# Chunked attention followed by a two-layer channel MLP: W1 loaded in four column quarters, an earlier release of the values loads, copies of turned keys and queries spread over steps, and the last tile computed by columns

## The chip, the cores and the metric

The kernel runs on one core of one Trainium2 chip. The metric is the device time of one execution in microseconds (us), as the median of several executions.

## What is computed

q, k and v have 4 batches, 8 heads, 768 positions and 64 features, in float32. First comes attention in chunks of 32 queries; each chunk sees 8 memory keys of its head, 16 positions to its left, itself, and 8 positions to its right. The heads are then put side by side (x has 4 x 768 rows of 512), and an MLP over a layer norm is added to x:

```
for c in range(nc):                       # 24 chunks of 32 queries
    l_start, r_end = max(0, c_start - 16), min(S, c_end + 8)
    k_full = concat([mem_k, k[:, :, l_start:r_end]])
    v_full = concat([mem_v, v[:, :, l_start:r_end]])
    scores = scale * q_c @ k_full^T
    out[:, :, c_start:c_end] = softmax(scores) @ v_full
...
xn = (x - mean(x)) / sqrt(var(x) + 1e-06) * g_ln
out = x + relu(xn @ w_ch1) @ w_ch2        # w_ch1 512 x 2048, w_ch2 2048 x 512
```

## The kernel before

**Tiles and units.** The 3072 rows of x are cut into 24 tiles of 128 rows, six to a batch. Three tiles make a unit, so there are eight units. The loop over the units is at L464. One unit is 16 "up" steps and then 12 "down" steps. An up step (L302) makes 128 of the 2048 hidden features for all 384 rows: four matmuls of 384 columns, one for each block of 128 input features, and a relu that puts the result into the tile rT. The relu of an even step runs on VectorE (L315), that of an odd step on ScalarE (L313). A down step (L319) does four of the 16 matmuls that make one output tile, each with 512 columns. After the fourth part, VectorE scales the sum by rstd and adds x (L331), and SyncE stores the tile (L334, 256 KB). The layer norm's factor rstd goes in only there; the matmuls work on (x - mean) * g.

**Attention is woven into the steps of the unit before.** While unit u runs, the attention of unit u+1's tiles is worked out. The dictionary `plan`, filled by `at(step, function, ...)` (L469), says after which step a piece of it is issued, and `attend` (L472) places three pieces for each tile. `scores` (L224) is eight matmuls of 128 columns and two exponentials on ScalarE (L237); `values` (L243) is 16 matmuls and VectorE's normalisation (L256 to L266); `turn_x` (L281) is four transposes on TensorE and a copy into xT on ScalarE (L289). `root` (L270), a square on ScalarE and a power on GpSimd, comes one step after `turn_x`.

**Turning keys and queries.** Scores need keys and queries with the features on the partitions. `kq_block` (L206) does this for two pairs of heads: 32 transposes for the keys and 32 for the queries on TensorE (L176, 16 for one pair of heads), then the copies out of PSUM, those of the keys by VectorE into KT (`keep_k`, L191), those of the queries by ScalarE into QZ (`keep_q`, L201). All copies of a block are issued together, keys of both pairs first, then queries of both. Batch 0 is special: its first 64 row groups of 96 are turned at the head of the program, a pair of heads at a time (L426 to L441), and the remaining third in unit 0 (steps 11 and 14). Batch 1 is turned in unit 1 (steps 2 and 6), batches 2 and 3 in units 2 and 4 (steps 19 and 22).

**PSUM.** There are two slots named att, of two banks each, and four named mm, of one bank. `slot` (L80) hands them out in turn. A matmul that is to write a slot waits until the slot's last reader is done.

**What sets the order.** Each engine runs its instructions in the order in which the program writes them (`manual_schedule`, L39). Waits between engines are put in by the framework, from which bytes of which tile an instruction reads and writes. GpSimd (POOL) issues all loads that change the type from float32 to float16: keys and queries (`load_kq`), values (`load_v_group`, `load_v_head`), W1 (`load_w1`), W2 (`load_w2`) and the memory values of batches 1 to 3. Each of these issues occupies POOL for 0.5 to 1.5 us; from the ninth on, each first waits for the landing of the eighth load before it. SyncE (SP) issues the loads and copies that keep the type: the memory keys and values, `v_mem`, `v_around`, the row g_row with g_ln, and the stores.

**The head of the program.** VectorE writes the zeros and ones that QZ, KT and V need (`clear_q` L341, `clear_k` L337, `clear_v` L344; the last ends with two copies from the tile `counts`, which put the mask of the first and the last window into V). The loads of V into a tile wait for `clear_v` of that tile. The order of loads on POOL is: first 64 row groups of K and Q of batch 0 in four loads; V groups 0 to 3 and 4, 5; W1's columns 0 to 512, 512 to 1024 and 1024 to 2048 (L399 to L401); the memory values; the remaining 32 row groups ("tails") of K and of Q; W2's blocks 0 and 1; V groups 6, 7; W2's block 2; V groups 8 to 11; W2's block 3. W1 lies in two tiles `w1c` of 1024 columns each. `stay_busy` (L294) issues matmuls on a tile of zeros between the first tiles' attention stages, whose results nobody reads.

Of the kernel before, what the change touches and what calls it, by code (L numbers as in the profile page):

```python
# [11 lines left out]
ALU = mybir.AluOpType  # L12
# [3 lines left out]
def kernel(  # L16
# [12 lines left out]
    nc = tc.nc  # L29
# [3 lines left out]
    NG = 12  # L33
# [59 lines left out]
    def as16(t):  # L93
        return t.bitcast(FP16)
# [4 lines left out]
    def load_kq(b, which, lo=0, hi=96, h0=0, h1=H):  # L99

        dst, src = ((k16, k), (q16, q))[which]
        nc.gpsimd.dma_start(
            out=dst[b % 2][lo:hi, h0:h1, :, :],
            in_=dram(src, (b * H + h0) * HS + 512 * lo,
                     [[512, hi - lo], [HS, h1 - h0], [1, 512]]),
        )
# [30 lines left out]
    def load_w1(lo, hi):  # L137
        c = lo // 1024
        nc.gpsimd.dma_start(
            out=w1c[c][:, :, lo - 1024 * c : hi - 1024 * c],  # L140
            in_=dram(moe_w_ch1, lo, [[FF, 128], [128 * FF, 4], [1, hi - lo]]),
        )

    def load_w2(c):

        nc.gpsimd.dma_start(
            out=w2c[c], in_=dram(moe_w_ch2, c * 512 * 512, [[2048, 128], [1, 2048]])
        )
# [48 lines left out]
    def keep_q(copy, pv, b, j, par, n, g0, g1):  # L197


        rows = slice(64 * par, 64 * par + 64)  # L200
        copy(  # L201
            out=free(QZ[b % 2][rows, j, g0, par, :], 0, [[128, g1 - g0], [8, 8], [1, 8]]),
            in_=free(pv[rows, :], 8 * g0, [[8, g1 - g0], [1, 8], [n, 8]]),
        )

    def kq_block(b, j, g0, g1, kind):  # L206

        pk, pq = slot("att"), None
        if kind == "att":
            pq = slot("att")  # L210
            pq = [pq[:, i, :] for i in range(2)]
        else:
            pq = [slot("mm")[:, :] for i in range(2)]
        for i in range(2):
            turn_kq(as16(pk[:, i, :]), k16[b % 2], j + i, 96)
        for i in range(2):
            turn_kq(as16(pq[i]), q16[b % 2], j + i, 96)
        for i in range(2):
            keep_k(as16(pk[:, i, :]), b, j + i, 96, g0 + 1 if g0 else 0, g1)
        for i in range(2):  # L220
            for par in range(2):
                keep_q(nc.scalar.copy, as16(pq[i]), b, j + i, par, 96, g0, g1)

    def scores(b, t):  # L224
        p = slot("att")
# [93 lines left out]
    def down(t, i, part):  # L319
# [9 lines left out]
        if part == 3:  # L329
# [3 lines left out]
            )  # L333
            nc.sync.dma_start(out=out[t // 6, 128 * (t % 6) : 128 * (t % 6) + 128, :], in_=o)  # L334


    def clear_k(i):  # L337
        nc.vector.memset(KT[i][:, :, 8:24], 0.0)
# [2 lines left out]
    def clear_q(i, par):  # L341

        nc.vector.memset(QZ[i][64 - 64 * par : 128 - 64 * par, :, :, par, :], 0.0)  # L343

    def clear_v(i):

        nc.vector.memset(V[i][0:32, 0, :, 0:64], 0.0)
        nc.vector.memset(V[i][64:96, NG - 1, :, 0:64], 0.0)
        nc.vector.memset(V[i][:, 1 : NG - 1, :, 64:65], 1.0)
        for c, g in enumerate((0, NG - 1)):  # L350
            nc.vector.tensor_copy(
                out=free(V[i][:, g, 0, 64:65], 0, [[HD, H]]),
                in_=free(counts[:, c : c + 1], 0, [[0, H]]),
            )
# [21 lines left out]
    nc.scalar.copy(out=memk16, in_=memk32)  # L376
    nc.scalar.copy(out=memv16[:, 0, :, 0:64], in_=memv32.rearrange("p (h d) -> p h d", h=H))
    stay_busy(10)
    for par in range(2):
        clear_q(0, par)  # L380
    clear_k(0)
    clear_v(0)
    mem_keys()
    mem_cols(0)
    stay_busy(5)
# [11 lines left out]
    nc.gpsimd.tensor_tensor(out=band[:, 1:2], in0=band[:, 1:2], in1=zero2[:, 1:2], op=ALU.add)  # L397
    for g in range(4, 6):
        load_v_group(0, g)  # L399
    load_w1(0, 512)  # L400
    load_w1(512, 1024)  # L401
    load_w1(1024, 2048)
    nc.gpsimd.dma_start(
        out=memv16[:, 1:B, :, 0:64],
        in_=dram(mem_v, H * 512, [[64, 8], [512, (B - 1) * H], [1, 64]]),
    )
    load_kq(0, 0, CUT, 96)
    load_kq(0, 1, CUT, 96)
    load_w2(0)
    load_w2(1)  # L410
    for g in range(6, 8):
        load_v_group(0, g)
    load_w2(2)
    for g in range(8, NG):
        load_v_group(0, g)
    load_w2(3)
# [29 lines left out]
    stay_busy(4)  # L446
    values(0, 0, 0)
    scores(0, 2)
    stay_busy(1)
    values(0, 1, 1)  # L450
    stay_busy(2)
    values(0, 2, 2)
    stay_busy(3)
    turn_x(0, 0, 0, "mm")
    stay_busy(4)
    turn_x(0, 1, 1, "mm")
    stay_busy(4)
    turn_x(0, 2, 2, "mm")
    for t in range(3):
        root(t, t)  # L460
# [3 lines left out]
    for u, tiles in enumerate(units):  # L464
        n = len(tiles)
        following = units[u + 1] if u + 1 < len(units) else []
        plan = {}

        def at(step, fn, *args):  # L469
            plan.setdefault(step, []).append((fn, args))  # L470

        def attend(steps):  # L472

            for i, (s0, s1, s2) in enumerate(steps):
                t = following[i]
                at(s0, scores, t // 6, t % 6)
                at(s1, values, t // 6, t % 6, t % 9)
                at(s2, turn_x, u + 1, i, t % 6)
                at(min(s2 + 1, 27), root, t % 6, t % 9)

        if u == 0:
            at(1, clear_q, 1, 0)
            at(5, clear_q, 1, 1)
            at(8, clear_v, 1)
            at(11, clear_k, 1)
            for j in (0, 2):
                at(11 + 3 * (j // 2), kq_block, 0, j, 6, NG, "att")
            for which in range(2):
                at(12, load_kq, 1, which)
            for g in range(6):  # L490
                at(15, load_v_group, 1, g)
            attend(((16, 19, 22), (17, 21, 24), (19, 23, 27)))
            at(26, mem_cols, 1)
            at(26, v_mem, 1)
        elif u == 1:
            for j in (0, 2):
                at(2 + 2 * j, kq_block, 1, j, 0, NG, "att")
            for g in range(6, NG):
                at(0, load_v_group, 1, g)
            for which in range(2):  # L500
                at(1, load_kq, 2, which)
            attend(((11, 16, 20), (15, 18, 23), (19, 22, 26)))
        elif following:
            steps = [(1 + 7 * i, 5 + 7 * i, 11 + 7 * i) for i in range(3)]
            if u in (2, 4):
                steps[2] = (15, 19, 22)
            attend(steps)
            if u in (2, 4):
                b = u // 2 + 1
                for j, step in ((0, 19), (2, 22)):  # L510
                    at(step, kq_block, b, j, 0, NG, "mm")
                for h in range(H):
                    at(2 + 2 * h, load_v_head, b, h)
                at(21, mem_cols, b)
                at(21, v_mem, b)
                at(22, v_around, b)
            if u == 3:
                for which in range(2):
                    at(2 + which, load_kq, 3, which)
        for step in range(16 + 4 * n):  # L520
            if step < 16:
                up(u, n, step)
            else:
                i, part = divmod(step - 16, 4)
                if u == 0:
                    d = step - 16
                    i, part = divmod(d, 2) if d < 6 else (d % 3, d // 3)
                down(tiles[i], i, part)
            for fn, args in plan.get(step, ()):
                fn(*args)  # L530

# [29 lines left out]
```

The softmax here doesn't subtract the row's maximum and nothing guards it: scores larger than these inputs give would overflow.

## Time and profile before

| | |
|---|---|
| median of 9 executions | 237.03 us (236.57 to 241.75) |
| the profiled execution: its own time | 237.09 us |
| its span, first to last instruction | 235.3 us |
| granted TensorE clock over the span | 0.996 |
| TensorE (PE) busy | 221.9 us, 94% |
| weight loads (PEld) busy | 135.9 us, 58% |
| VectorE (DVE) busy | 124.6 us, 53% |
| ScalarE (ACT) busy | 119.5 us, 51% |
| GpSimd (POOL) busy | 63.6 us, 27% |

By stretches of the span, TensorE is busy 9.9 of the first 12 us (of which much is the filler), 11.0 of the next 14, 32.6 of the 34 from 26 to 60, 48.3 of the 50 from 60 to 110, 49.4 of the 50 from 110 to 160, all of the 50 from 160 to 210, and 20.7 of the last 25.3.

How to read the profile's lines: L307 is line 307 of the kernel; PE is TensorE's matmuls, PEld its weight loads, which run beside the matmuls; "out<-in" names the tiles written and read. In a timeline line the first number is the start in us and the second the length of a group of instructions of one kind; the bracket tells how long the engine was idle just before and what ended that. In the list of waits, the three numbers are the total in us, the count, and the longest.

### The profile page before, as it was taken

The numbers are of one execution on the slowest core, as the hardware profiler recorded it, in microseconds if no ns is written. First come the engines' busy times: TensorE is split into PE (matmuls) and PEld (weight loads), VectorE is DVE, ScalarE is ACT, GpSimd is POOL, SyncE is SP. The second block draws the span as 40 slices with busy tenths as digits, with TensorE's granted clock in tenths as the row PEclk, the third lists the DMA queues.
The fourth block names the chain that finished last, engine by engine and source line by source line (L and its number), as shares of the span: only waits on it lengthen the run. The fifth ranks groups of instructions, "written<-read, shape, count | busy, mean of one in ns | idle before, by whom it ended". The sixth has DMA issues, their size and how long they took to land.

```text
span 235.3 us, 5407 instructions
## 1 busy us (share of the span) xinstructions
PE 221.9 (94%) x2251; PEld 135.9 (58%) x2251; DVE 124.6 (53%) x287; ACT 119.5 (51%) x227; POOL 63.6 (27%) x122
## 2 busy tenths in 40 slices
PE   7868999989899999989999999989999999999992
PEld 2544676547665577655764576656764676457540
DVE  6636773577735556384654365484644365434121
ACT  3663657455964456576572357576462457233200
POOL 6874156736400262303011344201011101110000
PEclk9999999999999999999999999999999999999998
DMA  4999999999998196942961193942001200110011
GB/s 77 193 126 208 201 193 175 169 201 225 106 153 171 49 119 12 73 88 54 201 109 45 51 120 10 94 64 92 0 3 45 89 3 0 46 57 34 0 71 64
DMA packets 44224, 22.30 MB, mean 95 GB/s; under 512 B 32376, under 2 KB 39928, under 8 KB 44152
## 3 DMA queue, kind: packets, MB, share of 16 engines
q0 software_dynamic: 39744, 14.38, 74.9%
q1 hardware_dynamic: 4456, 7.59, 10.7%
q8 instruction: 17, 0.28, 0.5%
q14 instruction: 7, 0.06, 0.1%
HBM read 29.10 MB, written 6.29 MB: 150 GB/s over the span
## 4 chain that ended last, share of the span: by engine, by line
PE 75%; DMA 9%; DVE 6%; issue 5%; ACT 3%; DVEq 0%
PE mm L307 33%; PE mm L324 30%; DMA w1c<-in_moe_w_ch_dram 6%; PE att L230 4%; PE att L176 3%; DMA V<-in_v_dram 3%; PE att L249 3%; DVE KT L191 2%; ACT QZ L201 2%; PE att L284 2%; DVE QZ L343 1%; DVE osb L331 1%; DVE xs L257 1%; PE mm L176 1%; ACT xT L289 0%
## 5 line engine op out<-in xcount | busy, mean ns | idle before, releaser
L307 PE MATMUL mm<-xT,w1c 128*128 128x384 f16 x512 | 90.3, 327 | 2.9 <-ACT xT L289 1.3
L324 PE MATMUL mm<-w2c,rT 128*128 128x512 f16 x384 | 89.0, 379 | 0.0
L307 PEld LDWEIGHTS <-w1c 128*128 128x128 f16 x512 | 56.1, 115 | 26.9 <-issue 2.1
L324 PEld LDWEIGHTS <-rT 128*128 128x128 f16 x384 | 35.6, 98 | 37.4
L315 DVE TENSOR_SCALAR rT<-mm 128x384 f16<-128x384 f32 x64 | 35.1, 556 | 33.0 <-PE mm L307 33.0
L313 ACT ACTIVATE rT<-mm 128x384 f16<-128x384 f32 x64 | 31.1, 490 | 40.3 <-PE mm L307 39.8
L331 DVE SCALAR_TENSOR_TENSOR osb<-mm,rstd,xs 128x512 f32<-128x512 f32 x24 | 18.0, 750 | 47.3 <-PE mm L324 25.9
L275 POOL TENSOR_SCALAR veps<-squares 128x1 f32<-128x1 f32 x24 | 4.6, 191 | 120.3 <-ACT junk L272 120.0
L237 ACT ACTIVATE AT<-att,band 96x512 f16<-96x512 f32 x48 | 30.1, 678 | 9.8 <-PE att L230 9.8
L289 ACT COPY xT<-att 128x512 f16<-128x512 f16 x21 | 12.3, 584 | 32.4 <-PE att L284 32.3
L112 POOL DMA_DIRECT2D V<-in_v_dram x24 | 18.5, 773 | 14.4 <-DMA V<-in_v_dram 5.2
L191 DVE COPY KT<-att 128x80 f16<-128x80 f16 (+3 forms) x44 | 18.3, 483 | 2.4 <-PE att L176 2.4
L266 DVE SCALAR_TENSOR_TENSOR xn<-xs,nmean,g_row 128x512 f16<-128x512 f32 x24 | 18.0, 752 | 0.9
L272 ACT ACTIVATE junk<-xs,nmean 128x512 f16<-128x512 f32 x24 | 17.4, 726 | 0.1
L257 DVE SCALAR_TENSOR_TENSOR xs<-att,rec 128x512 f32<-128x512 f32 x24 | 16.6, 692 | 0.8
L201 ACT COPY QZ<-att 64x384 f16<-64x384 f16 (+1 forms) x20 | 12.0, 601 | 8.4 <-PE att L176 8.1
L201 ACT COPY QZ<-mm 64x768 f16<-64x768 f16 (+1 forms) x18 | 13.6, 758 | 4.6 <-PE mm L176 4.4
L230 PE MATMUL att<-QZ,KT 128*128 128x128 f16 x192 | 14.9, 219 | 0.4 <-ACT QZ L201 0.2
L249 PEld LDWEIGHTS <-AT 96*64 96x64 f16 x384 | 8.6, 110 | 11.1 <-issue 5.3
L230 PEld LDWEIGHTS <-KT 128*128 128x128 f16 x192 | 12.6, 98 | 3.7 <-issue 0.7
L256 DVE RECIPROCAL rec<-att 128x8 f32<-128x8 f32 x24 | 4.9, 204 | 17.1 <-PE att L249 15.2
L279 POOL TENSOR_TENSOR rstd<-veps,mhalf 128x1 f32<-128x1 f32 x24 | 13.3, 554 | 2.0
(56 smaller groups left out, 132.3 us busy)
## 6 DMA issues: line engine op xcount, KB each, us to landing
out_dram<-osb SPq DMA_DIRECT2D x24, 256.0 KB, 2.4
V<-in_v_dram POOLq DMA_DIRECT2D x36, 96.0 KB, 7.3
k<-in_k_dram POOLq DMA_DIRECT2D x3, 768.0 KB, 10.5
q<-in_q_dram POOLq DMA_DIRECT2D x3, 768.0 KB, 13.1
w2c<-in_moe_w_ch_dram POOLq DMA_DIRECT2D x4, 512.0 KB, 13.5
w1c<-in_moe_w_ch_dram POOLq DMA_DIRECT2D x2, 512.0 KB, 9.2
w1c<-in_moe_w_ch_dram POOLq DMA_DIRECT2D x1, 1024.0 KB, 14.4
k<-in_k_dram POOLq DMA_DIRECT2D x3, 256.0 KB, 5.9
```

Source lines behind the costliest of these rows:

```text
L112: nc.gpsimd.dma_start(out=V[b % 2][r : r + hi - lo, g, :, 0:64], in_=dram(v, b * H * HS + lo * D, [[64, hi - lo], [HS, H], [1, 64]]),)
L191: copy(out=free(KT[b % 2], j * KC + 24 + 32 * ga + 8 * lo, [[KR, gb - ga], [8, m], [1, 8]]), in_=free(pv, lo, [[8, gb - ga], [1, m], [n, 8]]),
L201: copy(out=free(QZ[b % 2][rows, j, g0, par, :], 0, [[128, g1 - g0], [8, 8], [1, 8]]), in_=free(pv[rows, :], 8 * g0, [[8, g1 - g0], [1, 8], ...
L230: nc.tensor.matmul(out=p[:, gg, 128 * j : 128 * j + 128], lhsT=KT[b % 2][:, j, KR * g : KR * g + 128], rhs=QZ[b % 2][:, j, g, :, :], start ...
L237: nc.scalar.activation(out=free(a, 32 * c, [[512, 2], [64, 8], [1, 32]], KR), in_=free(p, 32 * c, [[512, 2], [64, 8], [1, 32]], KR), func= ...
L257: nc.vector.scalar_tensor_tensor(out=x.rearrange("p (h d) -> p h d", h=H), in0=free(p, 0, [[128, H], [1, 64]]), scalar=1.0, in1=free(r, 0, ...
L266: nc.vector.scalar_tensor_tensor(out=xn[i], in0=x, scalar=nmean[i], in1=g_row, op0=ALU.add, op1=ALU.mult,)
L307: nc.tensor.matmul(out=p, lhsT=free(w, i, [[4, 128]]), rhs=xT[u % 2][:, dt, 0 : 128 * n], start=(dt == 0), stop=(dt == 3),)
L313: nc.scalar.activation(out=o, in_=p, func=ACTF.Relu)
L315: nc.vector.tensor_scalar(out=o, in0=p, scalar1=0.0, scalar2=None, op0=ALU.max)
L324: nc.tensor.matmul(out=p, lhsT=rT[hc][:, 128 * i : 128 * i + 128], rhs=w2c[hc // 4][:, hc % 4, :], start=(hc == 0), stop=(hc == 15),)
L331: nc.vector.scalar_tensor_tensor(out=o, in0=p, scalar=rstd[t % 9], in1=xs[t % 9], op0=ALU.mult, op1=ALU.add,)
```

## The change

1. **W1 by quarters.** Three of W1's four column quarters are loaded first, then the tails of K and Q, then the fourth quarter. Then come W2's blocks 0, 1 and 2, V groups 6 and 7, the memory values, V groups 8 to 11, and W2's block 3. The tiles `w1c` stay as they are.
2. **Clears.** `clear_v(0)` goes to the front of VectorE's clears; `clear_q(0, 0)` is put between its memsets and its two copies from `counts`; then `clear_q(0, 1)` and `clear_k(0)`.
3. **Filler.** The counts of `stay_busy` after the third scores become 3, 3, 2, 2, 2 in place of 1, 2, 3, 4, 4.
4. **Copies of turned keys and queries.** `kq_block` issues the copies of its first pair of heads only (keys, then queries); those of the second pair are issued by `keep_rest`, placed by the plan. In unit 0 the blocks stand at steps 10 and 12 (were 11 and 14) with the rest at 11 and 13; in unit 1 at 2 and 8 (were 2 and 6) with the rest at 4 and 10; in units 2 and 4 at 19 and 23 (were 19 and 22) with the rest in the same step.
5. **Steps of attention.** In unit 0 the third `turn_x` goes from step 27 to 26; in unit 1 the first scores go from step 11 to 13.
6. **Last tile by columns.** The last output tile is made by `down_last`: for columns 0 to 256, 256 to 384 and 384 to 512, each time 16 matmuls, a VectorE step and a store.

```
-        for i in range(2):
+
+        def keep(i):
             keep_k(as16(pk[:, i, :]), b, j + i, 96, g0 + 1 if g0 else 0, g1)
-        for i in range(2):
             for par in range(2):
                 keep_q(nc.scalar.copy, as16(pq[i]), b, j + i, par, 96, g0, g1)
+
+        keep(0)
+        kept_later.append(lambda: keep(1))
+
+    kept_later = []
+
+    def keep_rest():
+        kept_later.pop(0)()
...
+    def down_last(t, i):
+
+        o = osb[t % 3]
+        for lo, hi in ((0, 256), (256, 384), (384, 512)):
+            p = slot("mm")[:, 0 : hi - lo]
+            for hc in range(16):
+                nc.tensor.matmul(
+                    out=p, lhsT=rT[hc][:, 128 * i : 128 * i + 128],
+                    rhs=w2c[hc // 4][:, hc % 4, lo:hi],
+                    start=(hc == 0), stop=(hc == 15),
+                )
+            nc.vector.scalar_tensor_tensor(
+                out=o[:, lo:hi], in0=p, scalar=rstd[t % 9], in1=xs[t % 9][:, lo:hi],
+                op0=ALU.mult, op1=ALU.add,
+            )
+            nc.sync.dma_start(
+                out=out[t // 6, 128 * (t % 6) : 128 * (t % 6) + 128, lo:hi], in_=o[:, lo:hi]
+            )
...
-    def clear_v(i):
+    def clear_v(i, between=lambda: None):
...
         nc.vector.memset(V[i][:, 1 : NG - 1, :, 64:65], 1.0)
+        between()
         for c, g in enumerate((0, NG - 1)):
...
-    for par in range(2):
-        clear_q(0, par)
+    clear_v(0, lambda: clear_q(0, 0))
+    clear_q(0, 1)
     clear_k(0)
-    clear_v(0)
...
-    load_w1(0, 512)
-    load_w1(512, 1024)
-    load_w1(1024, 2048)
+    for c in range(3):
+        load_w1(512 * c, 512 * c + 512)
+    load_kq(0, 0, CUT, 96)
+    load_kq(0, 1, CUT, 96)
+    load_w1(1536, 2048)
+    load_w2(0)
+    load_w2(1)
+    load_w2(2)
+    for g in range(6, 8):
+        load_v_group(0, g)
     nc.gpsimd.dma_start(
         out=memv16[:, 1:B, :, 0:64],
         in_=dram(mem_v, H * 512, [[64, 8], [512, (B - 1) * H], [1, 64]]),
     )
-    load_kq(0, 0, CUT, 96)
-    load_kq(0, 1, CUT, 96)
-    load_w2(0)
-    load_w2(1)
-    for g in range(6, 8):
-        load_v_group(0, g)
-    load_w2(2)
...
-    stay_busy(1)
+    stay_busy(3)
     values(0, 1, 1)
+    stay_busy(3)
+    values(0, 2, 2)
     stay_busy(2)
-    values(0, 2, 2)
-    stay_busy(3)
     turn_x(0, 0, 0, "mm")
-    stay_busy(4)
+    stay_busy(2)
     turn_x(0, 1, 1, "mm")
-    stay_busy(4)
+    stay_busy(2)
...
-                at(11 + 3 * (j // 2), kq_block, 0, j, 6, NG, "att")
+                at(10 + j, kq_block, 0, j, 6, NG, "att")
+                at(11 + j, keep_rest)
...
-            attend(((16, 19, 22), (17, 21, 24), (19, 23, 27)))
+            attend(((16, 19, 22), (17, 21, 24), (19, 23, 26)))
...
-                at(2 + 2 * j, kq_block, 1, j, 0, NG, "att")
+                at(2 + 3 * j, kq_block, 1, j, 0, NG, "att")
+                at(4 + 3 * j, keep_rest)
...
-            attend(((11, 16, 20), (15, 18, 23), (19, 22, 26)))
+            attend(((13, 16, 20), (15, 18, 23), (19, 22, 26)))
...
-                for j, step in ((0, 19), (2, 22)):
+                for j, step in ((0, 19), (2, 23)):
                     at(step, kq_block, b, j, 0, NG, "mm")
+                    at(step, keep_rest)
...
-                down(tiles[i], i, part)
+                if following or i < n - 1:
+                    down(tiles[i], i, part)
+                elif part == 0:
+                    down_last(tiles[i], i)
```

## The prediction

> **What bounds the kernel now.** I read the page first, then what TensorE waited for, the timeline around each wait, and the loads' times to landing.
>
> ```profile
> span 235.3 us, 5407 instructions
> ...
> PE 221.9 (94%) x2251; PEld 135.9 (58%) x2251; DVE 124.6 (53%) x287; ACT 119.5 (51%) x227; POOL 63.6 (27%) x122
> ```
>
> TensorE is the bound; a change can win only where it stands still. After the first up step these are nearly all of its stops (TensorE's list of waits: total, times, longest):
>
> ```profile
> PE mm L307 <- ACT xT L289: 1.3, 2, 0.7
> PE att L176 <- DVE KT L191: 1.2, 2, 0.6
> PE mm L307 <- ACT rT L313: 1.1, 1, 1.1
> ...
> PE mm L307 <- DMA w1c<-in_moe_w_ch_dram: 0.5, 1, 0.5
> ...
> PE att L230 <- ACT QZ L201: 0.2, 1, 0.2
> ```
>
> Their places, in the timeline (start, us, engine, line):
>
> ```profile
> 28.96 2.79 PE L307 MATMUL mm<-xT,w1c 128*128 128x384 f16 x16 [0.49 <-DMA w1c<-in_moe_w_ch_dram]
> ...
> 52.46 2.11 PE L307 MATMUL mm<-xT,w1c 128*128 128x384 f16 x12 [0.67 <-ACT xT L289]
> ...
> 60.30 3.21 ACT L201 COPY QZ<-att 64x768 f16<-64x768 f16 x4
> ...
> 64.07 0.81 PE L307 MATMUL mm<-xT,w1c 128*128 128x384 f16 x4 [1.09 <-ACT rT L313]
> ...
> 103.25 0.87 PE L176 MATMUL att<-identity,k 96*64 96x96 f16 x32 [0.60 <-DVE KT L191]
> ```
>
> The bracket counts from the modelled end of the last matmul. What a stop costs is counted from where the next matmul would have started, and is some 0.17 us more: 16 up matmuls from 60.19 take 2.60 (chain of waits), so the one at 64.07 was due at 62.79 and lost 1.28. In the same way the stops lost 0.84 (52.46), 0.39 (38.82, on QZ), 0.77 twice (103.25 and 155.41).
>
> W1's loads, the first weights' wait, and times to landing of W1:
>
> ```profile
> 12.36 1.53 POOL L139 DMA_DIRECT2D w1c<-in_moe_w_ch_dram  x2
> ...
> 14.54 0.74 POOL L139 DMA_DIRECT2D w1c<-in_moe_w_ch_dram  x1 [0.64 <-DMA V<-in_v_dram]
> ...
> 23.02 1.22 PE L307 MATMUL mm<-xT,w1c 128*128 128x384 f16 x6 [0.67 <-ACT xT L289]
> 23.23 0.80 PEld L307 LDWEIGHTS <-w1c 128*128 128x128 f16 x6 [0.98 <-DMA w1c<-in_moe_w_ch_dram]
> ```
>
> ```profile
> DMA to landing us min/median/max: 8.3/10.0/14.4
> ```
>
> So W1's quarters 1 and 2 land at 12.36+8.3 = 20.65 and 13.14+10.05 = 23.19, its second half at 14.54+14.4 = 28.91. The row at 23.23 matters most: step 0 uses columns of quarter 1 alone, there since 20.65, yet its second weight load went only when quarter 2 had landed. A load covers four row blocks of a 1024-column tile, and the program's tracking takes all between its first and last byte as written; only the first row block's weights escape. In the changed program's own list of waits it is the same: step 8's first weight load waits for quarter 3, its second for quarter 4.
>
> **The change part by part.** Positive is later.
>
> *W1 and the tails.* Step 8 now needs quarters 3 and 4, and between them POOL issues the tail rows of K and Q. Loads on this queue land in the order of issue. The tails' rows of before:
>
> ```profile
> 16.37 0.59 POOL L102 DMA_DIRECT2D k<-in_k_dram  x1 [0.43 <-DMA V<-in_v_dram]
> ...
> 17.56 0.58 POOL L102 DMA_DIRECT2D q<-in_q_dram  x1 [0.60 <-DMA V<-in_v_dram]
> ```
>
> With longest times to landing of 14.4 and 14.5 they land at 30.7 and 32.1; what was issued before them (memv, 15.27+14.0) at 29.3, so both take 2.75. Upper: all of before's second half, then the tails: 28.91+2.75 = 31.66. Lower: each quarter takes quarter 2's 2.54: 23.19+2.54+2.75+2.54 = 31.0. I take 31.3. One matmul (0.16) of step 8 runs ahead of the wait, so step 8 moves from 28.96 to an effective 31.35-0.16 = 31.19: **+2.23** (1.9 to 2.6; to 3.2 if rates sag). Each load waits for the landing of the eighth before it, on POOL too, but those all land by 20.7. W2's blocks come no later than 2.5 us before their steps, and V groups 6 and 7, now behind a third W2 block, at about 40, three us ahead; memv is first read by an SP copy near 52. All nothing, under the later PE.
>
> *Values released sooner, clears reordered.* V's first load now waits for the first count copy, some 1.9 us earlier (6.83 to about 5). But the queue is full of queries: the four K/Q loads land at 5.5, 7.3, 8.6, 10.3, and V comes behind them. So no gain. SP's memory values and g_row go out 1.7 sooner; of their 0.36 MB nothing had moved in 6 to 9 us, all in 9 to 12:
>
> ```profile
> q1 hardware_dynamic: 241, 0.36, 57.0%
> ```
>
> Now they may pass in front of the second K and Q loads and push the last Q to about 12.4. By the rows that follow it (scores +2, three chains of VectorE at about 2 us each) the third xT comes at 23.9 for 23.0. Either way step 8 is reached at 28.3 to 29.2, before 31.3: hidden under the W1 wait. The cover ends if the first up step starts after 25.9. Twelve filler matmuls between the tiles for fourteen: at most -0.2, under the same cover.
>
> [...] TensorE will stand 2 to 3 us at step 8. In this trace it was busy only 0.23 to 0.69 us in each of the microseconds 16 to 19, and the granted clock stayed 1.00, so I charge nothing. [...]
>
> *Unit 0.* kq_block moves from steps 11, 14 to 10, 12, and ScalarE copies half, does a relu, copies the other half. The second block's query transposes wait for all four copies: 0.11+2x0.48, relu 0.49, 2x0.48 = 2.53 after the first block, and TensorE is there at 2x0.65+0.72 = 2.02; with 0.06 to pass on, **+0.57** that was not there. Scores come later after the second block (2.81 against 1.51): the QZ stop goes, **-0.39**. turn_x at 26 puts a down step (0.86) over the xT copy (0.59): **-0.84**. Bounds: -1.23 (no new stop) to 0.
>
> *Unit 1.* Blocks at 2 and 8, halves two steps apart. ScalarE after a block: 1.6 of copies, relu, 1.6, relu; the relu that step 7 needs is ready at 2.2, TensorE comes at 2.6. The 1.28 goes. New: scores, five steps (3.25) behind the second block, need the last copies at 3.82+0.06 and the keys' at 3.43: 0.46. Net **-0.82** (-1.28 to 0). The second batch's queries (40.99+13.7 = 54.67) are there long before.
>
> *Units 2 and 4.* Only the second block's step changes, 22 to 23; halves in the same step leave ScalarE's order but for a root (0.9) now ahead of the copies. KT's copies end at 103.20, TensorE now comes at 102.48+0.86 = 103.34: **-1.54** for both (bounds -1.54 to 0). QZ is then ready near 108.3, scores at 109.8. v_around and v_mem keep their place on SP.
>
> *Last tile by columns.*
>
> ```profile
> 230.79 0.75 DVE L331 SCALAR_TENSOR_TENSOR osb<-mm,rstd,xs 128x512 f32<-128x512 f32 x1 [2.61 <-PE mm L324]
> ```
>
> Matmuls: 0.108 each for 256 columns (512 take 0.216), 0.056 for 128 (eight L230 in 0.45): 16x(0.108+0.056+0.056) = 3.52 against 3.46, +0.06. If each 128-column matmul took as long as its weight load (98 ns), 32x0.042 = +1.34 more; L230 has such loads too and runs at 56, so I take 56. The last VectorE step: 512 elements 0.75, about 0.22 of it fixed, so 128 about 0.35: -0.40 (-0.33 to -0.55). The last store is 64 KB in place of 256: it landed in 2.0, at 191 KB in half a us; 0 to -0.5, I take -0.3. Sum **-0.64** (-1.0 to +1.0). [...]
>
> Sum: 2.23+0.57-0.39-0.84-0.82-1.54-0.64 = -1.43. The profiled execution took 237.09 (235.3 and 1.8 around it), 0.06 over the median of 237.03. **Forecast 235.7.**
>
> **Rivals.**
> 1. *The split does what it says*: step 8 waits for quarter 3 alone (25.7), so the unit starts at the pace of xT, step 8 at 29.3 (+0.35 for +2.23): 233.8. The row at 23.23 speaks against it. 3%.
> 2. *The last tile runs at the weight loads' pace*: +1.34, 237.0, no difference. PE's weight-load rows of 98 ns speak for it, L230's pace against. 11%.
> 3. *W1's last quarter later still*, at 32.2 for 31.3: 236.6, no difference. The queue moved 166 to 199 KB/us in 26 to 31, 204 to 213 just before; 9%.
> 4. *Slower*: the stand at step 8 lowers the clock. While it is half, X us of work cost X/2 more; from X = 2.9 the gain is gone, from 4.3 it is slower, at 6.8 it is 239.1. For it: three such us of standing occur nowhere in the trace. Against: 16 to 19 us. 7%.
>
> **How the numbers follow.** The forecast, with its terms inside their bounds, has 62%: 234.6 to 236.2. Nothing is left below 234.6 but rival 1 and a late-end gain; upward the range takes rivals 2 and 3, and some 0.4 for such of the new orders' waits as I did not find (8%; a KT-like stop costs 0.77): 234.6 to 237.4. Within 0.3% (0.71 us, about what a measurement of this kernel can tell) fall rivals 2 and 3: 0.20. Slower: rival 4 and the waits not found, if they take back all: 0.15. Faster: 0.65.
>
> **What would show it.** In the profile after: a TensorE stop of 2 to 3 us on W1 near 29 to 31; W1's fourth load landing at 31.0 to 31.7; no stops at KT in units 2 and 4, none on a relu in unit 1; a new stop of some 0.6 on QZ copies in unit 0 and 0.4 at the first scores of unit 1; the last VectorE step near 0.35. The prediction is wrong if step 8 starts by 29.5 or after 32.5, if the clock row dips near 30, or if the last 48 matmuls take 4.5 us or more.

## The result and the profile after

The changed kernel takes 235.51 us in the median of 17 executions (234.54 to 236.92). The kernel before, run beside it, takes 237.5 (54 executions). The ratio is 0.9913, with a 95% interval of 0.9891 to 0.9935: the change is faster by 0.9%. The forecast was 235.7, inside a range of 234.6 to 237.4. Every ratio here is to the kernel before, run beside the kernel on the same chip, and leaves out executions more than 1.5% above the fastest of their kernel, while medians and ranges are of all executions.

The profiled execution took 236.57 us, some 1 us above that median. These are the lines of its page for the span, the engines and the granted clock (40 slices of 5.87 us, in tenths):

```profile
span 234.9 us, 5475 instructions
...
PE 224.0 (95%) x2281; PEld 138.9 (59%) x2281; DVE 124.9 (53%) x289; ACT 118.7 (51%) x227; POOL 64.3 (27%) x123
...
PEclk9979979999999999999999999999999999999998
```

The clock row has two dips, near 12 to 15 us and near 32 to 35; the kernel before had none in its profile but the one in the last slice, which both have. TensorE's list of waits (total, times, longest) has lost the stops on KT, on the relu and one of the two on xT, and has a new first entry:

```profile
PE mm L315 <- DMA w1c<-in_moe_w_ch_dram: 1.9, 1, 1.9
...
PE mm L315 <- ACT xT L297: 0.7, 1, 0.7
...
PE att L176 <- ACT QZ L201: 0.2, 1, 0.2
```

The same places in TensorE's timeline (start, length, what; the bracket is the idle time in front):

```profile
22.96 5.82 PE L315 MATMUL mm<-xT,w1c 128*128 128x384 f16 x33 [0.67 <-ACT xT L297]
30.73 2.45 PE L315 MATMUL mm<-xT,w1c 128*128 128x384 f16 x11 [1.95 <-DMA w1c<-in_moe_w_ch_dram]
33.11 1.49 PE L176 MATMUL att<-identity,k 96*64 96x96 f16 x32
...
54.78 2.11 PE L315 MATMUL mm<-xT,w1c 128*128 128x384 f16 x12
...
67.22 0.78 PE L238 MATMUL att<-QZ,KT 128*128 128x128 f16 x8
```

Step 8 (line L315 is the former L307) stands at 30.73, as forecast, waiting for W1's fourth quarter. Behind it 11 matmuls take 2.45 us where 11 of the same kind take 1.98 in the second profile below. The clock of the stretches (the column before the last two):

```profile
28.00:32.00 4.00, 2.05 (x13) 1.24 (x12) 2.00 (x3) 0.49 (x1) 1.72 (x3) 1.00 1.15 219
32.00:36.00 4.00, 4.00 (x71) 3.05 (x70) 3.07 (x13) 0.68 (x2) 0.77 (x1) 0.57 1.07 210
```

By single microseconds the clock is 0.54 in 32 to 33, 0.50 in 33 to 35 and 0.75 in 35 to 36: half speed for about 3.4 us, starting 1.4 us after the stand had ended. If the stand drew it, the stand of 1.95 us cost more than itself; the experiments test that.

The same kernel was profiled a second time, in an execution of 235.11 us (span 233.4). It has the stand, but not the half-clock stretch behind it:

```profile
30.57 1.98 PE L315 MATMUL mm<-xT,w1c 128*128 128x384 f16 x11 [1.92 <-DMA w1c<-in_moe_w_ch_dram]
32.48 0.87 PE L176 MATMUL att<-identity,k 96*64 96x96 f16 x32
...
53.05 2.11 PE L315 MATMUL mm<-xT,w1c 128*128 128x384 f16 x12
```

With the starts of each unit's first up matmul, the span falls into stretches. Step 8 is counted from where its first matmul would stand (0.16 before the one that waited):

| stretch (us) | before | after, 1st profile | after, 2nd profile | change | forecast |
|---|---|---|---|---|---|
| start of the span to step 8 | 28.96 | 30.57 | 30.41 | +1.61 / +1.45 | +2.23 |
| step 8 to unit 1 | 23.50 | 24.21 | 22.64 | +0.71 / -0.86 | -0.66 |
| unit 1 | 28.70 | 27.75 | 28.03 | -0.95 / -0.67 | -0.82 |
| units 2 and 4 together | 55.80 | 54.45 | 54.45 | -1.35 | -1.54 |
| units 3, 5, 6 and unit 7's up steps | 83.22 | 83.24 | 83.24 | 0.0 | 0 |
| last three tiles and the end | 15.12 | 14.68 | 14.63 | -0.44 / -0.49 | -0.64 |
| span | 235.3 | 234.9 | 233.4 | -0.4 / -1.9 | -1.43 |

Units are counted from their first up matmul. The changes of the second profile follow the forecast's terms nearly one by one. The first profile differs from it in one row above all: 24.21 against 22.64 is 1.57 us of half clock. The times of the changed kernel's 28 executions (18 in this run, 10 in a later one) differ by as much: the nine with a mean granted clock of 0.990 or less have a median of 236.5 us, the six with 0.997 or more one of 234.9.

### The profile page after: what moved, and what is told of

It reads as the page before. It is cut to its first block, busy times and chain, and to the rows that moved or that the text cites. A ratio compares the mean times of both kernels' runs of the same rounds, so it can differ in the third digit from the quotient of the medians.

```text
span 234.9 us, 5475 instructions
## 1 busy us (share of the span) xinstructions
PE 224.0 (95%) x2281; PEld 138.9 (59%) x2281; DVE 124.9 (53%) x289; ACT 118.7 (51%) x227; POOL 64.3 (27%) x123
## 4 chain that ended last, share of the span: by engine, by line
PE 84%; DMA 10%; DVE 1%; ACT 1%; POOL 1%; issue 1%
PE mm L332 34%; PE mm L315 34%; DMA w1c<-in_moe_w_ch_dram 6%; PE att L238 4%; PE att L176 4%; DMA V<-in_v_dram 4%; PE att L257 3%; PE att L292 2%; PE mm L350 2%; PE mm L176 1%; POOL V L112 1%; ACT QZ L201 1%; DVE QZ L370 1%; ACT rT L321 0%; DVE V L375 0%
## 5 line engine op out<-in xcount | busy, mean ns | idle before, releaser
L315 PE MATMUL mm<-xT,w1c 128*128 128x384 f16 x512 | 90.7, 328 | 2.7 <-DMA w1c<-in_moe_w_ch_dram 1.9
L332 PE MATMUL mm<-w2c,rT 128*128 128x512 f16 x368 | 86.1, 379 | 0.0
L315 PEld LDWEIGHTS <-w1c 128*128 128x128 f16 x512 | 56.2, 115 | 26.9 <-DMA w1c<-in_moe_w_ch_dram 3.5
L332 PEld LDWEIGHTS <-rT 128*128 128x128 f16 x368 | 33.9, 98 | 34.8
L339 DVE SCALAR_TENSOR_TENSOR osb<-mm,rstd,xs 128x512 f32<-128x512 f32 x23 | 17.3, 751 | 44.9 <-PE mm L332 23.0
L238 PE MATMUL att<-QZ,KT 128*128 128x128 f16 x192 | 15.5, 227 | 0.2 <-ACT AT L245 0.2
L238 PEld LDWEIGHTS <-KT 128*128 128x128 f16 x192 | 13.4, 102 | 3.7 <-issue 0.9
L257 PEld LDWEIGHTS <-AT 96*64 96x64 f16 x384 | 8.1, 111 | 8.9 <-issue 4.0
```

The costliest lines, as they stand in the source:

```text
L238: nc.tensor.matmul(out=p[:, gg, 128 * j : 128 * j + 128], lhsT=KT[b % 2][:, j, KR * g : KR * g + 128], rhs=QZ[b % 2][:, j, g, :, :], start ...
L315: nc.tensor.matmul(out=p, lhsT=free(w, i, [[4, 128]]), rhs=xT[u % 2][:, dt, 0 : 128 * n], start=(dt == 0), stop=(dt == 3),)
L332: nc.tensor.matmul(out=p, lhsT=rT[hc][:, 128 * i : 128 * i + 128], rhs=w2c[hc // 4][:, hc % 4, :], start=(hc == 0), stop=(hc == 15),)
L339: nc.vector.scalar_tensor_tensor(out=o, in0=p, scalar=rstd[t % 9], in1=xs[t % 9], op0=ALU.mult, op1=ALU.add,)
```

## The experiments

The questions were two. Does the stand at step 8 itself lower the clock? And what is the stand worth: is taking it away a gain, or does it only hide the next wait? Three sets of kernels ran, each beside the kernel before on a chip of its own, so kernels of different sets are compared by their ratios and not by their times.

**Fillers in the stand.** Edit of the changed kernel:

```
             at(8, clear_v, 1)
+            at(7, stay_busy, 8, att[0][:, 0, :])
```

> Eight filler matmuls of 512 columns (8 x 0.216 = 1.73 us) are put behind step 7 of unit 0, into the stand of the changed kernel at step 8. Theory A, the stand lowers the clock: step 8 still starts at 30.5 to 30.8, the half-clock stretch that the changed kernel's profile has from 32.1 to 35.5 us is gone, mean granted clocks are 0.992 or higher in all executions, and the profiled span is some 1.7 us under 234.9 (about 233.2); the median falls by 0.3 to 1.0 to 234.5 to 235.2, since only a part of the executions had the stretch. Theory B, the stretch has another cause (the loads' traffic or chance): clocks near 0.983 turn up again, and the median stays at 235.5 within 0.3.

Measured: median 235.07 (234.49 to 235.28, 6 executions), ratio 0.9864 [0.9823, 0.9906]. No mean clock is under 0.992. Its stretches:

```profile
28.00:32.00 4.00, 3.71 (x21) 1.96 (x19) 1.92 (x3) 0.49 (x1) 2.08 (x3) 1.00 1.17 214
32.00:36.00 4.00, 4.00 (x94) 2.91 (x93) 3.33 (x14) 2.11 (x5) 0.77 (x1) 1.00 1.06 212
```

TensorE was busy 3.71 us of 28 to 32 in place of 2.05, W1's quarter landed no sooner (30.8), and the clock stayed at 1.00. The span is 233.4, as in the second profile of the changed kernel. This fits theory A. Of 28 executions of the changed kernel nine had a mean clock of 0.990 or less; here none of six had. The gain in time is not shown by the ratio alone, since the interval overlaps the changed kernel's (0.9891 to 0.9935). One new line stands in its timeline:

```profile
55.38 0.87 PE L176 MATMUL att<-identity,k 96*64 96x96 f16 x32
56.60 0.87 PE L176 MATMUL att<-identity,q 96*64 96x96 f16 x32 [0.35 <-DMA q<-in_q_dram]
```

Without the half clock TensorE came 1.4 us sooner to the queries of batch 1, and waited for their load, which landed at 56.56. That led to the second question.

**A longer stand.** If the stand draws the half clock, a longer one should draw it in every execution. Edit of the changed kernel:

```
-    load_w1(1536, 2048)
     load_w2(0)
+    load_w1(1536, 2048)
```

> The changed kernel with W1's fourth quarter behind W2's first block: it lands 2.5 us later, near 33.2, and the stand at step 8 grows from 1.95 to some 4.4 us. [...] Rival (the stretches come by chance, whatever the stand's length): some executions at 0.997 or more, median 237.3 to 238.3.

Measured: median 239.41 (238.26 to 241.32, 12 executions), ratio 1.0061 [1.0028, 1.0094]; mean clocks 0.975 to 0.993, none higher. Its wait, in the timeline, and the clock behind it, by stretches:

```profile
33.63 3.29 PE L315 MATMUL mm<-xT,w1c 128*128 128x384 f16 x11 [4.86 <-DMA w1c<-in_moe_w_ch_dram]
```

```profile
34.00:36.00 2.00, 2.00 (x8) 0.96 (x7) 1.04 (x2) 0.00 (x0) 0.64 (x1) 0.50 1.08 217
```

Eleven matmuls took 3.29 us for 1.98. No execution of the 12 was free of half clock, as it has to be if the stand draws it; of the 28 of the changed kernel, six were. A mean clock of 0.993 is one block of 3.4 us, and in those executions it can't be told from the block at the head. The next kernel settles it.

**Fillers at both stands.** To the fillers of the first kernel five more are added at the head, where TensorE waits 1.2 us for the last queries of batch 0:

```
+    stay_busy(5, spare)
     for j in range(2, 4):
         turn_kq(first_q[j], q16[0], j, CUT)
```

> The changed kernel with eight filler matmuls behind step 7 of unit 0 and five more at the head, where TensorE waits 1.2 us for the last queries. Theory A (both half-clock stretches come from stands): mean clocks 0.997 or more in all executions, median 234.3 to 234.9, spread under 0.8. Rival: the stretch at 11.6 to 15 us stays, clocks 0.992, median 235.1.

Measured: median 234.80 (234.35 to 235.78, 6 executions), ratio 0.9874 [0.9834, 0.9914], mean clocks 0.997 to 1.000. The clock row of its page:

```profile
PEclk9999999999999999999999999999999999999999
```

Clocks of 0.997 or more: six of six here, six of 28 in the changed kernel. With the stands filled, the half clock is gone: theory A. The time is another matter. The spread was 1.43 us for the forecast's 0.8, and the ratio is not better than with the first fillers alone (0.9864). That fits a stretch at the head that lies under the wait for W1, but is not shown further.

**The order of loads alone.** The kernel before with the change's clears, order of loads and filler counts (items 1 to 3 of the change).

```
-    load_w1(0, 512)
-    load_w1(512, 1024)
-    load_w1(1024, 2048)
+    for c in range(3):
+        load_w1(512 * c, 512 * c + 512)
+    load_kq(0, 0, CUT, 96)
+    load_kq(0, 1, CUT, 96)
+    load_w1(1536, 2048)
...
```

> The kernel before with the order of clears, the order of loads and the filler counts of the change, and nothing else of it. Theory A: step 8 goes from 28.96 to 30.6 to 30.8 (+1.6 to +1.8), a part of the executions has a half-clock stretch of 3.4 us behind it (+1.7); the QZ stop of 0.39 may go. Median 238.3 to 239.8, ratio 1.005 to 1.012: slower. Rival (the earlier values loads and clears give something that the changed kernel's other parts do not need): 237.0 to 237.5, no change.

Measured: median 240.42 (238.34 to 242.71), ratio 1.0085 [1.0042, 1.0127]: a loss by itself, with a ratio inside theory A's range and a median above it. Its wait:

```profile
31.19 4.07 PE L307 MATMUL mm<-xT,w1c 128*128 128x384 f16 x15 [2.68 <-DMA w1c<-in_moe_w_ch_dram]
```

So the first three items are paid for by the others. Unit 1 of this profile also holds a stop of 2.25 us for which the profile names no cause; it is left open.

**No stand: all four quarters first.** Edit of the changed kernel:

```
-    for c in range(3):
+    for c in range(4):
         load_w1(512 * c, 512 * c + 512)
     load_kq(0, 0, CUT, 96)
     load_kq(0, 1, CUT, 96)
-    load_w1(1536, 2048)
```

> All four quarters of W1 are issued before the tails of K and Q. Theory A (step 8 waits for the landing of the fourth quarter, and nothing else was lost at it): the fourth quarter lands near 28.2 to 28.5, step 8 starts at 28.7 to 28.9 with no stand and no half clock behind it; tails land at 29.6 and 30.9, before the first block's transposes at 30.7 and 31.4; span 1.7 to 2.0 under that of an undipped changed kernel, median 233.4 to 233.9, ratio to before 0.984 to 0.986. Rival: the tails land later than 31.5 and the stand moves to step 10; then the median is 234.5 to 235.5.

Measured: median 236.95 (234.82 to 240.05), ratio 0.9903 [0.9862, 0.9944]. The stand is gone and the time is not better than the changed kernel's 0.9913. The profiled execution took 239.66 us, far over the median, so its sizes are not those of the median; it shows where the gain can go, not that every execution loses it there. TensorE's waits from 22 to 62 us:

```profile
PE att L176 <- DMA q<-in_q_dram: 3.0, 1, 3.0
PE mm L332 <- DMA w2c<-in_moe_w_ch_dram: 1.1, 1, 1.1
PE mm L315 <- ACT xT L297: 0.7, 1, 0.7
PE mm L315 <- DMA w1c<-in_moe_w_ch_dram: 0.5, 1, 0.5
```

and its timeline:

```profile
58.73 0.87 PE L176 MATMUL att<-identity,q 96*64 96x96 f16 x32 [2.97 <-DMA q<-in_q_dram]
59.54 5.77 PE L315 MATMUL mm<-xT,w1c 128*128 128x384 f16 x24
```

Step 8 passed at 28.7 with next to no wait, unit 0 went on to 48.8 with two stops of some 0.3, and then TensorE stood for W2's last block and for the queries of batch 1. The 3 us there were followed by slow matmuls too: 24 took 5.77 us for 4.09, what 3.4 us of half clock would cost.

**No stand: W1 in four tiles.** Edit of the changed kernel (the load and `up` follow):

```
-    w1c = [sb.tile([128, 4, 1024], FP16, name=f"w1c{i}") for i in range(2)]
+    w1c = [sb.tile([128, 4, 512], FP16, name=f"w1c{i}") for i in range(4)]
```

> W1 lies in four tiles of 512 columns in place of two of 1024; the order of loads is the changed kernel's. Theory A (the wait at step 8 comes from two quarters sharing a tile): step 8 waits for the third quarter alone (landed 25.8), starts at 28.7 to 28.9, no stand, step 12 comes after 31.5 and finds the fourth quarter landed at 30.7; median 233.4 to 233.9. Rival (the wait is in the landing itself, or all weights of a unit are waited for): step 8 stays at 30.5 to 30.8 and the median at 235.5.

Measured: median 237.90 (235.26 to 240.04), ratio 0.9942 [0.9899, 0.9985]. The list of waits from 22 to 40 us has no line on W1 any more, at step 0 or at step 8, with the changed kernel's order of loads; below it is the start of unit 0 in the timeline:

```profile
PE mm L315 <- ACT xT L297: 0.7, 1, 0.7
PE mm L292 <- DVE xn L274: 0.4, 1, 0.4
PE att L176 <- ACT QZ L201: 0.2, 1, 0.2
...
22.85 7.31 PE L315 MATMUL mm<-xT,w1c 128*128 128x384 f16 x44 [0.67 <-ACT xT L297]
```

Its 44 matmuls, steps 0 to 10, run in one piece and are over at 30.16; the fourth quarter landed at 31.16. That shows the mechanism of the forecast: a quarter waited for its neighbour only because both lie in one tile. And it refutes the time of theory A. As in the kernel before this one, the stop comes back on W2's last block (1.2) and on q (2.7), again in an execution over its median (239.07).

**No stand, and later use of the next loads.** To the order with four quarters first: the memory values go behind W2's last block, and unit 1 turns its keys and queries later.

```
-                at(2 + 3 * j, kq_block, 1, j, 0, NG, "att")
-                at(4 + 3 * j, keep_rest)
+                at(5 + 2 * j, kq_block, 1, j, 0, NG, "att")
+                at(7 + 2 * j, keep_rest)
...
-            attend(((13, 16, 20), (15, 18, 23), (19, 22, 26)))
+            attend(((15, 17, 21), (16, 19, 24), (19, 22, 26)))
```

> The order with all four quarters of W1 first, the memory values behind W2's last block, and unit 1's blocks of keys and queries at steps 5 and 9 (the rest of their copies at 7 and 11; scores at 15, 16, 19, values at 17, 19, 22, transposes of x at 21, 24, 26). Theory B (without the stand at step 8 TensorE ran into the loads of W2's last block and of batch 1's queries): with some 2 us more until the queries are used, the stop on q of 3.0 falls to 1 or less, and the gain of the missing stand shows: median 233.5 to 235.0. Theory A2 (the stand was no loss at all: the loads' queue sets the end of unit 1's start whatever stands before it): the stop moves on to the values or back to W2's last block and the median stays at 235.5 or above.

Measured: median 234.94 (233.06 to 236.09, 6 executions), ratio 0.985 [0.9795, 0.9905]; profiled at 233.47, span 231.8. Unit 1 starts at 51.72 (the changed kernel: 53.05 in its better profile), and the queries no longer stop it:

```profile
51.72 4.06 PE L315 MATMUL mm<-xT,w1c 128*128 128x384 f16 x24
55.72 0.87 PE L176 MATMUL att<-identity,k 96*64 96x96 f16 x32
56.42 0.85 PE L176 MATMUL att<-identity,q 96*64 96x96 f16 x32
```

This fits theory B: the stand was a loss, but taking it away pays only if the loads behind it are used later too. It is not proven by the times, since the interval overlaps the changed kernel's (0.9891 to 0.9935), and the two edits (memory values, steps of unit 1) were not tried apart. Nor is the half clock gone: two of the six executions have mean clocks of 0.982 and 0.983.

**Units 2 and 4 alone.** Edit of the kernel before:

```
-                for j, step in ((0, 19), (2, 22)):
+                for j, step in ((0, 19), (2, 23)):
```

> The kernel before with one number changed: in units 2 and 4 the second block of keys and queries stands at step 23 in place of 22. By the prediction's term the two stops of TensorE on KT (0.77 us lost each, at 103.25 and 155.41 in the kernel before) go and no other comes: -1.54, ratio about 0.9935. By the changed kernel's profile the two units gave 0.67 each: -1.33, ratio 0.9944. Rival: the copies end later and the scores of the next unit wait for QZ: between -0.5 and 0.

Measured: median 235.93 (235.28 to 240.79), ratio 0.9903 [0.9862, 0.9945]. In the profile units 2 and 4 take 27.23 each for 27.90, so -0.67 and not the -0.77 forecast, and nothing came back later. The interval of the ratio holds both forecasts, and the whole change's 0.9913 too: by the time alone, this one changed number can't be told from the whole change. The end of the gap, and something else in unit 1, in the timeline:

```profile
55.72 0.87 PE L176 MATMUL att<-identity,q 96*64 96x96 f16 x32 [0.45 <-DMA q<-in_q_dram]
...
103.02 1.03 PE L324 MATMUL mm<-w2c,rT 128*128 128x512 f16 x4
103.97 0.87 PE L176 MATMUL att<-identity,k 96*64 96x96 f16 x32
```

The down step lasts 0.86, so the transposes were due at 103.88 and started at 103.97. That 0.1 is the passage from 512-column matmuls to small ones, which other such places of the trace have too (97.49 + 0.86 = 98.35, next start 98.44); the forecast left it out. The wait on q is in work that this edit does not touch: the same load landed at 55.67 here and at 54.67 in the kernel before. The slack of 0.5 us that the kernel before had there is thus not there in every execution.

**The last tile alone.** The kernel before with `down_last` and its call.

> The kernel before with the last tile by columns alone. From the first of the last 48 matmuls to the end of the span the kernel before took 8.2 us and the changed kernel 7.77: -0.4 is expected, ratio 0.998 (the prediction said -0.64). In the profile: the last VectorE step 0.35 for 0.75, the last matmuls later by 0.1. Rival: the last matmuls run at the pace of the weight loads, 4.5 us or more for 3.5, and the time is the same or longer.

Measured: median 236.76 (235.61 to 239.31), ratio 0.9945 [0.991, 0.998]. From unit 7's first down matmul to the end: 14.26 us, 15.12 in the kernel before, -0.86. The changed kernel had -0.44 and -0.49 there. In both kernels the last 48 matmuls take 3.70 us and the last VectorE step is 0.35 long, and SP makes the difference. First the changed kernel's last two VectorE steps, then its three stores and this kernel's (durations in ns, min/median/max):

```profile
230.04 0.35 DVE L355 SCALAR_TENSOR_TENSOR osb<-mm,rstd,xs 128x128 f32<-128x128 f32 x1 [0.42 <-PE mm L350]
230.87 0.35 DVE L355 SCALAR_TENSOR_TENSOR osb<-mm,rstd,xs 128x128 f32<-128x128 f32 x1 [0.47 <-PE mm L350]
```

```profile
L359 SPq DMA_DIRECT2D out_dram<-osb x3: 332/383/1177, 229.6 to 231.7; - x3
```

```profile
L352 SPq DMA_DIRECT2D out_dram<-osb x3: 332/332/637, 230.9 to 232.5; - x3
```

The second store keeps SP for 1.18 us in the changed kernel (1.19 in its second profile) and for 0.64 here. The third is ready 0.8 us behind it, so only in the changed kernel it has to queue: it goes out 0.47 us after its VectorE step, here 0.03. What makes the second store so long is open.

**The copies of units 0 and 1 alone.** The kernel before with items 4 and 5 of the change, without units 2 and 4.

> The kernel before with the spread copies and the new steps of units 0 and 1 alone (units 2 and 4 as before, W1 as before). Theory A (TensorE's stops are the cost): the QZ stop (0.39), the xT stop (0.84) and the relu stop (1.28) go, stops of 0.2 to 0.3 come at the second block of unit 0 and at unit 1's scores: -1.9, ratio 0.992. Theory B (the queue of loads is a floor in units 0 and 1): TensorE reaches the queries of batch 1 some 1.0 us sooner than in the kernel before, which had 0.5 us to spare there, and waits for them 0.3 to 1.5 us: -0.5 to -1.5, with a stop on the load of q in unit 1 in the profile.

Measured: median 237.04 (235.59 to 242.22), ratio 0.9948 [0.9909, 0.9987]. Unit 1 took 27.75 for 28.70, -0.95 as in the changed kernel. There was no stop on q, but that says nothing on theory B: TensorE ran unit 0 2.6 us late, because the granted clock was half at the head:

```profile
17.00:18.00 1.00, 0.36 (x15) 0.36 (x14) 0.41 (x1) 0.29 (x1) 0.64 (x2) 0.54 1.50 183
18.00:23.00 5.00, 5.00 (x39) 2.21 (x34) 3.53 (x10) 0.59 (x1) 2.39 (x4) 0.50 1.22 210
```

So this run leaves theory B undecided for the kernel before. It shows what the forecast's row (16 to 19 us in the kernel before, little busy and yet at 1.00) could not: here waits for V of the same kind (0.5 and 0.7 us, in front of 16.70 and 17.64) were followed by 6.8 us of half clock.

**Everything together.** The kernel without the stand, with five more fillers at the head and the last tile in two pieces:

```
-        for lo, hi in ((0, 256), (256, 384), (384, 512)):
+        for lo, hi in ((0, 384), (384, 512)):
```

> All four quarters of W1 first, memory values behind W2's last block, unit 1's blocks at steps 5 and 9, five more fillers at the head, and the last tile in two pieces (columns 0 to 384 and 384 to 512) in place of three. In the changed kernel's profile the second of the three stores kept SP for 1.18 us and the last store went out 0.47 after its VectorE step; with two pieces it should follow at once: -0.4. Fillers at the head: no half clock there. Median 233.0 to 234.3, ratio to before 0.979 to 0.984. Rival: the first piece's larger store lands last and nothing is won at the end; and the loads' queue takes back what the head gains: 234.5 to 235.0.

Measured: median 234.70 (232.50 to 237.03, 6 executions), ratio 0.9827 [0.9772, 0.9881]. The median lies in the rival's range, the ratio in the forecast's. At the end SP follows at once:

```profile
L359 SPq DMA_DIRECT2D out_dram<-osb x2: 332/332/332, 231.1 to 231.8; - x2
```

The end takes 14.39 us, which is no better than the three pieces at their best (14.26). The profiled execution (236.78) again waited for batch 1's queries, 2.26 us, though they were used at the later step: they landed at 58.52, against 55.77 in the profile of the kernel without these two edits.

**The changed kernel again**, beside the last three:

> The changed kernel itself once more, beside the three kernels below on the same chip: 235.5 within 0.5, mean clocks from 0.983 to 1.000.

Measured: median 235.76 (234.66 to 236.64, 10 executions), ratio 0.9913 [0.9879, 0.9947]; its profile is the second one above. On this chip the medians are 235.76 for the changed kernel, 234.80 with fillers at both stands and 234.70 for everything together. The last has the best ratio and the shortest execution, but a wide spread (4.5 us, for 1.4 with the fillers). The intervals of the three ratios overlap, so this order of the kernels is likely and not shown.

## Why the prediction was right, step by step

The sign, the size and the mechanism held: a loss of some 1.5 us at W1, bought back by removed stops. The time agrees closer (235.51 for 235.7) than the terms, because two errors had opposite signs: W1's wait was put too dear by 0.6 to 0.8, and a half clock that costs 1.57 in a part of the executions was put at nothing. That closeness is luck.

- **W1 and the tails: mis-sized.** "I take 31.3", and +2.23: the fourth quarter landed at 30.68 and 30.52 in the two profiles, so +1.61 and +1.45, both under the lower bound of 1.9. The tails took about what was forecast (2.68 and 2.97 from the third quarter's landing to the queries', for 2.75). The third and fourth quarters were faster: together 4.66 us (2.47 and 2.19) and 4.71 (2.89 and 1.82), under even the best case, twice 2.54.
- **The clock: the failed step.** "The granted clock stayed 1.00, so I charge nothing." The stand at step 8 drew 3.4 us of half clock in some executions, which cost 1.57 us in the first profile; the fillers took it away. The first profile's clock row shows the prediction's own sign of being wrong, a dip near 30. The case was there as rival 4, but with 7% and as the way to "slower"; in truth it comes in a part of the executions, and there, with X = 3.4, it takes back 1.57 of a gain of 1.9, near its X/2 of 1.7. The row of 16 to 19 us says little of a full stand: TensorE worked 0.23 us or more in each of its microseconds. The kernel before does hold a stand of three us, at its end: the last matmul is over at 230.70, and the granted clock, 1.00 until 233.5, is 0.50 from 234 on. In the changed kernel less was enough: a stand of 1.95 us in the first profile, while one of 1.92 in the second was not.
- **Loads used late: a cover taken for granted.** "The second batch's queries are there long before" was wrong. In the kernel before they landed at 54.67 and their transposes began at 55.20, 0.5 us later. In the changed kernel the stand brought TensorE to them late enough, in the second profile by 0.04 us (landed at 55.76, used at 55.80), so the error stayed hidden; the two kernels without the stand made it visible.
- **Unit 0:** the new stop on QZ was 0.34 (transposes begun at 35.39 took 1.04 for 0.70 in the second profile) for 0.57; the stops on QZ (0.39) and xT (0.84) went. Sum -0.86 where the clock held, for -0.66.
- **Unit 1:** -0.95 and -0.67 for -0.82. The stop on the relu went, and the new loss at the scores was there, 0.33 for 0.46 (20 matmuls from 63.81 end near 67.06, the scores begin at 67.22 and hold TensorE for 0.62 in place of 0.45). The second profile lost 0.25 more in the transposes at 61.33, for which its list of waits names no cause.
- **Units 2 and 4:** -1.35 for -1.54, by the passage of 0.1 each.
- **Last tile:** -0.44 and -0.49 for -0.64. VectorE's last step came out at 0.35 as forecast. Matmuls of 128 columns ran near the 56 ns taken from L230's row: VectorE's last two steps start 0.83 us apart (230.04, 230.87), 16 matmuls at 52 ns. What was missed is SP's queue of stores, 0.44 us; without it the last tile alone gave -0.86, more than forecast.
- **Head:** first up step at 22.96 and 23.13 for 23.02: hidden, as forecast.

Rival 1 (the split lets step 8 go after the third quarter) is refuted for the changed kernel: its step 8 waits for the fourth; with separate tiles it does go. Rival 2 (weight loads' pace) is refuted by the 3.70 us of the last 48 matmuls. Rival 3 (the quarter later still) went the other way.

## What to carry to other kernels

A wait that one removes on a saturated load queue is a loan: here the 1.95 us at W1 gave way to 2.97 or 2.72 on batch 1's queries and 1.11 or 1.18 on W2's last block. Look up which loads come behind it, and by how much each is ahead of its use, before the gain is booked. A stand of TensorE can have two prices, its length and a half clock behind it (1.95 us and 1.57 in the first profile); here work that filled it, even useless work, took away the second. And where a load is split to let the first part go early, the parts need tiles of their own: in one tile step 8 waited 1.95 us for the quarter that it does not use, in tiles of their own not at all.

## What the runs showed of the hardware

The half clock came in blocks of 3.4 us. From the mean clocks of single microseconds, the changed kernel's two blocks run from 11.6 to 15.0 and from 32.1 to 35.5, and those of the kernel with the longer stand from 12.5 to 15.9 and from 33.0 to 36.4. In both the starts are 20.5 us apart, about six times the length of a block. The 6.8 us in the kernel with the copies alone are two such lengths in a row.

The busy share alone does not decide whether a block follows. In the first profile of the changed kernel TensorE was busy 1.45 of the 3.4 us ahead of the second block (28.7 to 32.1, 43%), and 1.87 of the 3.4 ahead of the one at the head (8.2 to 11.6, 55%). By its timeline the same stretch around the stand holds some 1.5 us of work in the second profile as well, and there the clock is 1.00 from 30 to 36. What decides it is not shown.

The 16 DMA engines were in the mean over 90% busy in every half microsecond from 18 to 38 us, in the kernel before (first) and in the changed one (second; view of the DMA engines over that stretch):

```profile
DMA  9999999999999999999999999999999999999999
...
DMA packets 4283, 4.00 MB, mean 200 GB/s; under 512 B 2197, under 2 KB 3423, under 8 KB 4280
```

```profile
DMA  9999999999999999999999999999999999999999
...
DMA packets 4545, 4.10 MB, mean 205 GB/s; under 512 B 1937, under 2 KB 4158, under 8 KB 4542
```

What stays open is why the queries of batch 1, behind the same bytes, land anywhere from 54.67 to 58.69 us. The stores of the first tiles ran beside that load, but they do not tell the cases apart: in the kernel with everything together the first went out at 50.54 and the queries landed at 58.52, in the kernel without these two edits at 50.82 and 55.77.
